# Clustered attention and two feed-forwards on one core: centroid similarities from split operands, fewer early weight conversions, and another order of feed-forward steps

## The chip, the cores and the metric

One core of a Trainium2 chip runs the whole kernel. The metric is the device time of one execution in microseconds (us); lower is better. The core has a matrix engine (TensorE, PE in the profile, with its weight loads listed apart as PEld), three engines for elementwise work (VectorE = DVE, ScalarE = ACT, GpSimd = POOL) and DMA queues that SyncE (SP) issues. TensorE accumulates into PSUM, a small memory of eight banks of 512 fp32 columns; everything else lies in SBUF.

## The reference

Shortened; all data are fp32 at the chip, except that the four weight matrices arrive as 64-bit floating-point numbers.

```
B, H, S, D = q.shape                        # 2, 8, 768, 64
q_n, k_n, c_n = (x / (norm(x) + 1e-06) for x in (q, k, centroids))   # written out in the source
q_assign = argmax(einsum('bhsd,hcd->bhsc', q_n, c_n), -1)            # 16 centroids per head
k_assign = argmax(einsum('bhsd,hcd->bhsc', k_n, c_n), -1)
scores = where(q_assign[..., :, None] == k_assign[..., None, :], q @ k.T / sqrt(D), -1e9)
attn = exp(scores - max(scores));  attn = attn / (sum(attn) + 1e-09)
x = (attn @ v) as [1536 tokens, 512]
h = x @ w_in;   x = maximum(0.01 * h, h) @ w_out                     # moe:  512 -> 2048 -> 512
h = x @ w_in2;  P = a0 + a1*h + a2*h^2 + a3*h^3;  Q = 1 + |b0|*|h| + |b1|*h^2
out = (P / (Q + 1e-06)) @ w_out2                                     # moe2: 512 -> 2048 -> 512
```

## The kernel before

**Numbers.** TensorE multiplies in a reduced form of fp32, fp32r, wherever exactness is kept another way: an operand is split into a high part (rounded to fp32r) and a low part (the rest), and a product of two fp32 matrices becomes three fp32r products: high·high, high·low and low·high. Names that end in h and l are such parts (`xh`, `xl`; `wih`, `wil`; `gh`, `gl`; `ph`, `pl`). The centroid similarities alone (`sims`, L307) are multiplied in plain fp32; each of their matmuls shows as two records in the trace.

**Attention** (`Attention.run`, about the first 281 us). Two heads make a pair, six tiles of 128 query rows a head, so a pair is 12 units and the eight pairs are 96. One iteration of the loop handles one new unit and several older ones, in fixed slots: maximum of the unit's scores on DVE (`row_max`, `nm`), normalisation of an older pair of units on POOL, two transposes into PSUM of the probabilities of the unit four iterations older (`pT` on PE), their high part on ACT (`ph`) and low part on DVE (`pl`), exponentials on ACT (`e`), scores of the next unit on PE (`s`), value products on PE (`o`, three units make a group), and at the end of a group an addition on DVE (`xf`) and, some iterations later, its split into `xh` and `xl` on POOL (`finish`).

Beside this the next pairs are prepared. Table `plan` in `prep_pieces` lists what a later pair needs, with an iteration (counted from that pair's first unit) and a slot of the iteration: loads of q and k, their transposes on PE into a PSUM tile `pa` (`trans`, L230), copies to `x` on ACT (`trans_out`, L233), splits into `hl` on POOL, similarities on PE, their copy `sv` on ACT, the maximum over the 16 centroids on DVE (`sims_max`, L335), one-hot rows, and the split of v into `vs` on POOL (`vsplit`, L394 and L395). The slots stand in the code where `go(...)` is called: "act" before the exponential, "pe" after the scores, "dve" after the low parts, "end" last. The transposes, the similarities and `pT` take turns in three PSUM tiles of one tag; two larger tiles hold scores, and one holds `o`.

**Weights.** A 64-bit weight chunk (`st`) becomes fp32 (`wf`, or `xst` in the first part of attention) by one ACT operation (`conv_a`, L767), one DVE shift (`conv_s`, L774) and two DVE combinations (`conv_c`, L780), and is then split by ACT (L787) and POOL (L790). In attention each iteration does one such small step at most, two iterations of three, for the four chunks that the first group of the first feed-forward needs (two of `wi`, two of `wo`). These chunks are saved to a DRAM scratch buffer and loaded again as plain fp32 at the end of attention.

**Feed-forwards.** 128 steps (n, j, f): a group of weights n, a block j of 384 tokens, a slice f of 128 hidden columns; steps 0 to 63 are the first (leaky), 64 to 127 the second (rational). `make_h(i)` is 12 matmuls of 384 columns into one of four `h` tiles, `back(i)` the product with `wo` into four accumulators `y0` to `y3`: 12 matmuls of 384 columns in the first feed-forward, 9 of 512 in the second. The loop body for step i does `back(i - 3)`, then `make_h(i)`, then the elementwise work of step i-1 and of i-2, then, where a block of a group ends, `collect(i - 3)`: additions on DVE that free the accumulators. In the second feed-forward the elementwise chain of a step goes ACT (`y`, `u`), POOL (`z`, twice), ACT (`ln`, `r`), DVE (`u`, `r`, `h`), ACT (`gh`), DVE (`gl`).

Engines take their instructions in the order of the program, and the order is written by hand (a manual schedule): an instruction that waits holds up what is behind it on its engine.

## Time and profile before

| | |
|---|---|
| time, three runs | 829.56, 830.09, 830.41 us (median 830.09) |
| profiled execution | 830.46 us, of which its span in the trace is 828.7 us |
| busy: PE, PEld | 797.1 us (96%), 740.7 us (89%) |
| busy: DVE, ACT, POOL | 649.1 us (78%), 533.3 us (64%), 398.8 us (48%) |
| granted TensorE clock, mean | 0.998 of full speed |
| moved by DMA | 79.80 MB, 96 GB/s over the span |

The span is cut into stretches by landmarks of the work: a pair of attention begins with the exponential of its first unit (60.67, 93.18, 124.27, ... us), the first feed-forward runs from about 281 to 545 us, the second to 825, and the last output lands at 828.7 us. Busy shares are means over stages with different limits, so the argument goes by stage. TensorE's records are pipelined: a record lasts longer than the distance to the next one, and the pace is read from the distances of starts.

### The profile page before, as it was taken

The page shows a single profiled execution, that of the slowest core. Times are in us where ns is not written, and L with a number is a line of the kernel's source. Part 1 is how long each engine was busy: PE and PEld are TensorE (multiplying, and loading weights), DVE is VectorE, ACT ScalarE, POOL GpSimd, SP SyncE. Part 2 cuts the span into 40 slices and gives each one's busy share as a digit, 9 for nine tenths or more (in the row PEclk, how much of TensorE's full clock was granted, in tenths as well). Part 3 has the DMA queues.
Part 4 walks back from the last instruction along what each step waited for, and adds up shares of the span by engine and source line. Part 5 has one row for each costly group of instructions (what it writes and reads, how often), then busy time and mean ns, then how long its engine had stood idle before and what let it go on. Part 6 is the DMA issues. An engine that isn't in the chain of part 4 may idle for free.

```text
span 828.7 us, 13356 instructions
## 1 busy us (share of the span) xinstructions
PE 797.1 (96%) x4545; PEld 740.7 (89%) x4545; DVE 649.1 (78%) x1232; ACT 533.3 (64%) x1131; POOL 398.8 (48%) x428
## 2 busy tenths in 40 slices
PE   5898999999999899999999999999999999999997
PEld 4887898898888899999999999997889888988995
DVE  6579989989999557766567556758888878888887
ACT  4588988988989544544253345447666667766664
POOL 5557877877665422331031024256555555554442
PEclk9999999999999999999999999999999999999999
DMA  3775745645410223435544454431111110100112
GB/s 102 175 207 116 169 103 117 170 97 124 106 36 26 102 85 120 131 124 169 165 147 155 141 189 130 150 89 27 35 30 28 38 39 26 26 1 1 40 39 76
DMA packets 42835, 79.80 MB, mean 96 GB/s; under 512 B 5392, under 2 KB 25360, under 8 KB 42768
## 3 DMA queue, kind: packets, MB, share of 16 engines
q1 hardware_dynamic: 42768, 78.96, 33.9%
q8 instruction: 36, 0.59, 0.3%
q14 instruction: 31, 0.25, 0.1%
HBM read 50.37 MB, written 10.49 MB: 73 GB/s over the span
## 4 chain that ended last, share of the span: by engine, by line
PE 50%; POOL 15%; DVE 14%; ACT 10%; issue 8%; DMA 2%; SPq 1%; POOLq 0%; DVEq 0%; ACTq 0%
PE y L961 18%; PE h L961 17%; POOL z L1013 6%; PE o L552 5%; PE pT L519 4%; POOL z L1010 4%; PE s L477 3%; DVE pl L538 3%; DVE nm L486 3%; ACT ln L1026 2%; PE sims L307 2%; ACT r L1027 2%; POOL wol L790 2%; POOL wil L790 2%; DMA st<-in_moe_w_in_dram 1%
## 5 line engine op out<-in xcount | busy, mean ns | idle before, releaser
L961 PE MATMUL h<-xh,wil 128*128 128x384 f32 x512 | 172.2, 336 | 0.0
L961 PE MATMUL h<-xh,wih 128*128 128x384 f32 x512 | 171.9, 336 | 0.0
L961 PE MATMUL h<-xl,wih 128*128 128x384 f32 x512 | 171.8, 336 | 0.0
L995 DVE TENSOR_TENSOR gl<-h,gh 128x384 fp32r<-128x384 f32 x128 | 70.8, 553 | 85.6 <-ACT gh L990 68.0
L511 POOL TENSOR_SCALAR e<-e,sum 128x768 f32<-128x768 f32 x96 | 88.6, 936 | 61.5 <-DVE sum L507 44.4
L790 POOL TENSOR_TENSOR wil<-wf,wih 128x512 fp32r<-128x512 f32 x32 | 41.6, 1308 | 143.8 <-ACT wih L787 143.8
L538 DVE TENSOR_TENSOR pl<-pT,ph 128x384 fp32r<-128x384 f32 x192 | 97.2, 545 | 16.6 <-ACT ph L532 15.5
L961 PEld LDWEIGHTS h<-xl,wih 128*128 128x128 f32 x512 | 96.2, 188 | 2.7
L961 PEld LDWEIGHTS h<-xh,wih 128*128 128x128 f32 x512 | 96.2, 188 | 2.5
L486 DVE TENSOR_REDUCE nm<-s 128x1 f32<-128x768 f32 x96 | 90.9, 947 | 7.3 <-PE s L477 6.8
L961 PEld LDWEIGHTS h<-xh,wil 128*128 128x128 f32 x512 | 96.2, 188 | 0.0
L999 ACT ACTIVATE h<-h 128x384 f32<-128x384 f32 x64 | 30.4, 476 | 98.6 <-PE h L961 98.6
L532 ACT CAST ph<-pT 128x384 fp32r<-128x384 f32 x192 | 82.4, 481 | 17.4 <-PE pT L519 16.2
L497 ACT ACTIVATE e<-s,nm 128x768 f32<-128x768 f32 x96 | 87.3, 909 | 9.4 <-DVE nm L486 5.8
L990 ACT CAST gh<-h 128x384 fp32r<-128x384 f32 x128 | 61.6, 482 | 40.4 <-DVE h L1034 38.3
L961 PE MATMUL y<-gh,woh 128*128 128x384 f32 x256 | 86.1, 336 | 0.1
L961 PE MATMUL y<-gl,woh 128*128 128x384 f32 x256 | 85.8, 335 | 0.2 <-DVE gl L995 0.2
L961 PE MATMUL y<-gh,wol 128*128 128x384 f32 x256 | 85.9, 336 | 0.0
L519 PE MATMUL pT<-ident,e 128*128 128x128 f32 x576 | 81.7, 278 | 2.7 <-DVE pl L538 2.7
L1010 POOL TENSOR_SCALAR z<-y,abv 128x384 f32<-128x384 f32 x64 | 43.2, 676 | 77.6 <-ACT y L1006 70.4
L961 PE MATMUL y<-woh,gh 128*128 128x512 f32 x192 | 76.6, 399 | 2.5 <-ACT gh L990 1.5
L961 PE MATMUL y<-woh,gl 128*128 128x512 f32 x192 | 76.6, 399 | 1.3 <-DVE gl L995 1.0
(104 smaller groups left out, 1855.3 us busy)
## 6 DMA issues: line engine op xcount, KB each, us to landing
st<-in_moe_w_in_dram SPq DMA_DIRECT2D x30, 512.0 KB, 4.6
st<-in_moe_w_out_dram SPq DMA_DIRECT2D x30, 512.0 KB, 4.6
a<-hl SPq DMA_DIRECT2D x56, 192.0 KB, 3.7
b<-hl SPq DMA_DIRECT2D x28, 192.0 KB, 6.0
wf<-scratch_wi SPq DMA_DIRECT2D x14, 256.0 KB, 3.1
wf<-scratch_wo SPq DMA_DIRECT2D x14, 256.0 KB, 3.1
qraw<-in_q_dram SPq DMA_DIRECT2D x16, 192.0 KB, 3.1
kraw<-in_k_dram SPq DMA_DIRECT2D x16, 192.0 KB, 3.2
```

What stands on the lines that cost most here:

```text
L486: nc.vector.reduce_max(un["nm"], un["s"][:, 0:S], axis=AX.X, negate=True)
L497: nc.scalar.activation(un["e"], un["s"][:, 0:S], AF.Exp, bias=un["nm"], accum_out=un["recip"])
L511: nc.gpsimd.tensor_scalar(un["e"], un["e"], un["recip"], 1.0, op0=ALU.mult, op1=ALU.mult)
L519: nc.tensor.transpose(pp[:, kt * P:(kt + 1) * P], un["e"][:, k0:k0 + P], ident)
L532: nc.scalar.copy(un["hi", part], un["pT", part])
L538: nc.vector.tensor_tensor(self.group[gi]["pl"][:, part * n:(part + 1) * n, i * P:(i + 1) * P], un["pT", part], f32(un["hi", part]), op=ALU ...
L790: nc.gpsimd.tensor_tensor(hold["l"][:, i:i + wr, :], hold["wf", i], f32(hold["h"][:, i:i + wr, :]), op=ALU.subtract,)
L961: nc.tensor.matmul(o, lhsT=l, rhs=r, start=(first and idx == 0), stop=(last and idx == n - 1),)
L990: nc.scalar.copy(d["gh"], d["h"])
L995: nc.vector.tensor_tensor(d["gl"], d["h"], f32(d["gh"]), op=ALU.subtract)
L1010: nc.gpsimd.tensor_scalar(d["z"], d["y"], abv[:, 1:2], abv[:, 0:1], op0=ALU.mult, op1=ALU.add)
L1013: nc.gpsimd.tensor_tensor(d["z"], d["z"], d["y"], op=ALU.mult)
```

## The change

1. **Similarities.** For the second to the eighth pair `sims` is replaced by `sims_split`: the centroids are split once into `cs` (two new POOL operations in the startup), and each of the six tiles of a head takes two fp32r matmuls: the high part of q or k against both parts of the centroids (64 columns), and its low part against the high part (32 columns, added to the first half). ACT copies 384 instead of 192 columns out of PSUM (`split_out`), and a new POOL operation adds the two halves (`add_sims`, L348). The first pair keeps plain fp32. In the second pair the maximum and the three steps behind it come one iteration later.
2. **Transposes of q and k** go to a new slot "pa", behind the value products and the low parts.
3. **Early weights.** Only the two `wi` chunks are still converted in attention and saved to scratch, one step every third iteration from the 15th on; the two `wo` chunks are loaded at the end of attention in their 64-bit form and converted there.
4. **End of attention.** The last two units have their own denominators; the last one is normalised by DVE instead of POOL, its transposes take a score tile, and the last group's `o` a tile of the tag `pT`.
5. **Feed-forward steps.** `make_h(i)` stands before `back(i - LAG)`.

```diff
--- before.py
+++ after.py
@@ -96,6 +96,7 @@
         nc.vector.tensor_tensor(abv, bv, nbv, op=ALU.max)
 
     cc = const.tile([P, H, 2, C], F32, name="cc")
+    cs = const.tile([P, H, 2, 2, C], F32R, name="cs")
 
     xh = {}
     xl = {}
@@ -189,6 +190,11 @@
+        def centroid_split(self):
+            gp = nc.gpsimd
+            gp.tensor_scalar(cs[:, :, 0], cc, 1.0, 1.0, op0=ALU.mult, op1=ALU.mult)
+            gp.tensor_tensor(cs[:, :, 1], cc, f32(cs[:, :, 0]), op=ALU.subtract)
+
         def centroid_zero(self):
             nc.gpsimd.memset(cc, 0.0)
 
@@ -312,6 +318,38 @@
                         stop=True,
                     )
 
+            def sims_split(h, tile_=self.ptile):
+                pp = tile_("sims")
+                st["pp"]["s", h] = pp
+                w = 4 * C
+                c4 = cs[:, g * HP + h].rearrange("p s u c -> p (s u c)")
+                for j in range(T):
+                    i, t = divmod(j, TH)
+                    sl = slice(t * P, (t + 1) * P)
+                    nc.tensor.matmul(
+                        pp[:, j * w:(j + 1) * w], lhsT=part(h, 0, i)[:, sl], rhs=c4,
+                        start=True, stop=False,
+                    )
+                    nc.tensor.matmul(
+                        pp[:, j * w:j * w + 2 * C], lhsT=part(h, 1, i)[:, sl], rhs=c4[:, 0:2 * C],
+                        start=False, stop=True,
+                    )
+
+            def split_out(h):
+                if h == 0:
+                    st["sv"] = tok.tile([P, HP, NS2, C], F32, tag="sv", name="sv")
+                st["s2"] = tok.tile([P, T, 2, 2 * C], F32, tag="s2", name="s2")
+                nc.scalar.copy(
+                    st["s2"],
+                    st["pp"].pop(("s", h))[:, 0:4 * C * T].rearrange("p (j s n) -> p j s n", j=T, s=2),
+                )
+
+            def add_sims(h):
+                gp.tensor_tensor(
+                    st["sv"][:, h].rearrange("p (j u) c -> p j (u c)", u=2),
+                    st["s2"][:, :, 0], st["s2"][:, :, 1], op=ALU.add,
+                )
+
             def sims_out(h):
                 if h == 0:
                     st["sv"] = tok.tile([P, HP, NS2, C], F32, tag="sv", name="sv")
@@ -398,30 +436,32 @@
             plan = [
...
-                (-23, "pe", trans, 0, 1),
+                (-23, "pa", trans, 0, 1),
...
-                (-15, "pe", sims, 1),
-                (-14, "act", sims_out, 1),
+                (-15, "pe", sims_split, 1),
+                (-14, "act", split_out, 1),
+                (-14, "end", add_sims, 1),
                 (-13, "dve", sims_max),
...
@@ -441,8 +481,9 @@
             if p == 0:
                 return []
             if p == 1:
-                late = {"sims": (-12, -10), "sims_out": (-11, -9), "sims_max": -9, "is_max": -9,
-                        "rank": -9, "first": -8, "onehot": (-7, -6)}
+                late = {"sims_split": (-12, -10), "split_out": (-11, -9),
+                        "add_sims": (-11, -9), "sims_max": -8, "is_max": -8,
+                        "rank": -8, "first": -7, "onehot": (-7, -6)}
                 done = ("load_qk", "trans", "trans_out", "split_hi", "split_lo", "place_a", "place_b")
                 moved = [
                     (-13, "end", place_b, 0),
@@ -498,21 +539,23 @@
                 un["e"], un["s"][:, 0:S], AF.Exp, bias=un["nm"], accum_out=un["recip"]
             )
 
-        def denom(self, u):
+        def denom(self, u, alone=False):
             un = self.unit[u]
-            nc.scalar.activation(un["sum"], un["sum"], AF.Identity, bias=eps)
-
-        def recip(self, u):
+            x = un["recip"] if alone else un["sum"]
+            nc.scalar.activation(x, x, AF.Identity, bias=eps)
+
+        def recip(self, u, alone=False):
             un = self.unit[u]
-            nc.vector.reciprocal(un["sum"], un["sum"])
-
-        def normalize(self, u):
+            x = un["recip"] if alone else un["sum"]
+            nc.vector.reciprocal(x, x)
+
+        def normalize(self, u, eng=nc.gpsimd):
             un = self.unit[u]
-            nc.gpsimd.tensor_scalar(un["e"], un["e"], un["recip"], 1.0, op0=ALU.mult, op1=ALU.mult)
+            eng.tensor_scalar(un["e"], un["e"], un["recip"], 1.0, op0=ALU.mult, op1=ALU.mult)
 
         def trans_p(self, u, part):
             un = self.unit[u]
-            pp = self.pq.tile([P, 512], F32, tag="pT", name="pT")
+            pp = self.ring("pT") if u == NU - 1 else self.ptile("pT")
             n = T // 2
             for kt in range(n):
                 k0 = (part * n + kt) * P
@@ -546,7 +589,10 @@
             p, h, half, _ = self.info(gi * QT)
             gr = self.group[gi]
             if a == 0:
-                gr["o"] = self.po.tile([P, BLK], F32, tag="o", name="o")
+                if (gi + 1) * QT == NU:
+                    gr["o"] = self.ptile("o")[:, 0:BLK]
+                else:
+                    gr["o"] = self.po.tile([P, BLK], F32, tag="o", name="o")
             for n in range(a, z):
                 kt, j = divmod(n, 2)
                 nc.tensor.matmul(
@@ -651,6 +697,7 @@
             assign(h0)
             for h in range(HP):
                 f0["vsplit"](h)
+            self.centroid_split()
             for h in range(HP):
                 halves(f1, h)
                 by_pool(f1, h)
@@ -681,7 +728,10 @@
                 go("dve0")
                 if 0 <= i < NU:
                     self.row_max(i)
-                if i % 2 == 0 and 0 <= i - 2 < NU:
+                if NU - 1 <= i <= NU:
+                    self.recip(i - 1, True)
+                    self.normalize(i - 1, (nc.gpsimd, nc.vector)[i - NU + 1])
+                elif i % 2 == 0 and 0 <= i - 2 < NU:
                     self.recip(i - 2)
                     self.normalize(i - 2)
                     self.normalize(i - 1)
@@ -696,7 +746,9 @@
                 go("act")
                 if 0 <= i < NU:
                     self.exp(i)
-                    if i % 2 == 1:
+                    if i >= NU - 2:
+                        self.denom(i, True)
+                    elif i % 2 == 1:
                         self.denom(i)
                 if 0 <= i + 1 < NU:
                     self.scores(i + 1)
@@ -706,6 +758,7 @@
                 if live:
                     self.lo(i - TL, 0)
                     self.lo(i - TL, 1)
+                go("pa")
                 if ok and r == QT - 1:
                     self.merge_add(gi)
                 go("dve")
@@ -713,13 +766,15 @@
                 if rd == 0 and 0 <= gd < n_groups:
                     self.finish(gd)
                 go("end")
-                if UP // 2 <= i < NU - 2 * UP and i % 3:
+                if i == UP // 2:
+                    fill[1].preload(4)
+                if UP + 3 <= i < NU - 2 * UP and i % 3 == 0:
                     fill[1].step()
                 if i == last_prep:
                     self.pc.close()
                     extra[0]()
                 elif i > last_prep:
-                    extra[1]()
+                    extra[1](i >= NU + TL)
 
     class Weights:
         def __init__(self, pools):
@@ -874,8 +929,8 @@
             else:
                 weights.add((which, n), weight_source(n, which), which, n % 2, WIDE)
 
-    def queue_scratch(n):
-        for which in ("wi", "wo"):
+    def queue_scratch(n, whiches=("wi", "wo")):
+        for which in whiches:
             src = weight_source(n, which)
             t = dram.tile([P, src.shape[1], src.shape[2] // WW], F32, name=f"scratch_{which}{n}")
             weights.add((which, n), src, which, n % 2, WIDE, store=t)
@@ -909,7 +964,7 @@
                 for j in range(NB // 2, NB):
                     slot(f"xh{j}")
                     slot(f"xl{j}")
-                queue_scratch(0)
+                queue_scratch(0, ("wi",))
 
         def open_weights(which, par, **kw):
             wpools[which, par] = wctx.enter_context(
@@ -924,8 +979,9 @@
             open_stage("wsta", side="right")
             queue_group(0)
 
-        def early_step():
-            weights.step(1)
+        def early_step(late):
+            if late or weights.waits_for(("wi", 0)):
+                weights.step(1)
 
         weights = Weights(wpools)
         with ExitStack() as actx:
@@ -1107,10 +1163,10 @@
                     if WIDE and n1 + NG - 1 > NG0 and n1 + NG - 1 < len(groups):
                         queue_scratch(n1 + NG - 1)
                     total = weights.pending()
+            if i < NS:
+                make_h(i)
             if i >= LAG:
                 back(i - LAG)
-            if i < NS:
-                make_h(i)
             if 0 <= i - 1 < NS:
                 start(i - 1)
             if 0 <= i - 2 < NS and rational(i - 2):
```

On TensorE, at the k transposes of the third pair's first head (`pa<-ident,kraw`; `s` are scores, `o` value products, `pT` probability transposes), the order before is:

```order
L477 MATMUL s<-a 128x512
L477 MATMUL s<-a 128x256
L477 MATMUL s<-b 128x512
L477 MATMUL s<-b 128x256
L230 MATMUL pa<-ident,kraw 128x128 x3
L552 MATMUL o<-ph,vs 128x384
L552 MATMUL o<-pl,vs 128x384
L552 MATMUL o<-ph,vs 128x384
L552 MATMUL o<-pl,vs 128x384
L519 MATMUL pT<-ident,e 128x128 x6
```

and of the change at the same place:

```order
L518 MATMUL s<-a 128x512
L518 MATMUL s<-a 128x256
L518 MATMUL s<-b 128x512
L518 MATMUL s<-b 128x256
L598 MATMUL o<-ph,vs 128x384
L598 MATMUL o<-pl,vs 128x384
L598 MATMUL o<-ph,vs 128x384
L598 MATMUL o<-pl,vs 128x384
L236 MATMUL pa<-ident,kraw 128x128 x3
L562 MATMUL pT<-ident,e 128x128 x6
```

The transposes now stand behind the four value products instead of ahead of them.

On POOL, in the iteration just before a pair's `sims_max` (`vs` is the split of v, `xh1` and `xl1` the split of a finished group, `e` a normalisation), the order before is:

```order
L394 TENSOR_SCALAR vs_1146<-vraw_983 128x6x64
L395 TENSOR_TENSOR vs_1146<-vraw_983,vs_1146 128x6x64
L587 TENSOR_SCALAR xh1_1178<-xf_756 128x384
L588 TENSOR_TENSOR xl1_1179<-xf_756,xh1_1178 128x384
L511 TENSOR_SCALAR e_1131<-e_1131,sum_1132 128x768
```

and of the change:

```order
L432 TENSOR_SCALAR vs_1186<-vraw_1012 128x6x64
L433 TENSOR_TENSOR vs_1186<-vraw_1012,vs_1186 128x6x64
L348 TENSOR_TENSOR sv_1035<-s2_1169 128x192
L633 TENSOR_SCALAR xh1_1218<-xf_782 128x384
L634 TENSOR_TENSOR xl1_1219<-xf_782,xh1_1218 128x384
L554 TENSOR_SCALAR e_1171<-e_1171,sum_1172 128x768
```

The new addition, whose result `sv` is what `sims_max` reads, stands behind the split of v and ahead of the split of the finished group.

On TensorE at the start of the first feed-forward, at the end of the third step's `h` (`h_3984`, in the change `h_4096`), the order before is:

```order
L961 MATMUL h_3984<-xl1_1179,wih_3492 128x384
L961 MATMUL h_3984<-xh1_1178,wil_3493 128x384
L961 MATMUL y0_4005<-gh_3977,woh_3950 128x384
L961 MATMUL y0_4005<-gl_3979,woh_3950 128x384
L961 MATMUL y0_4005<-gh_3977,wol_3951 128x384
```

and of the change:

```order
L1017 MATMUL h_4096<-xl1_1219,wih_3592 128x384
L1017 MATMUL h_4096<-xh1_1218,wil_3593 128x384
L1017 MATMUL h_4117<-xh1_1218,wih_3592 128x384
L1017 MATMUL h_4117<-xl1_1219,wih_3592 128x384
L1017 MATMUL h_4117<-xh1_1218,wil_3593 128x384
```

The fourth step's `h` now comes before the first step's `y`; the same shift by one block holds in every step that follows.

## Rows read from the trace of the kernel before

**Rows 1.** Busy time of the engines, whole span, from the page.

```profile
PE 797.1 (96%) x4545; PEld 740.7 (89%) x4545; DVE 649.1 (78%) x1232; ACT 533.3 (64%) x1131; POOL 398.8 (48%) x428
```

**Rows 2.** Windows: length; busy PE, PEld, DVE, ACT, POOL (instructions); clock, DMA, GB/s.

```profile
60.67:93.18 32.51, 30.37 (x211) 27.33 (x210) 31.13 (x57) 27.62 (x67) 24.68 (x28) 1.00 0.56 124
93.18:124.27 31.09, 30.26 (x214) 27.85 (x213) 28.22 (x52) 28.08 (x68) 23.74 (x28) 1.00 0.59 137
124.27:156.19 31.92, 30.49 (x207) 27.08 (x206) 31.15 (x58) 27.55 (x66) 23.52 (x27) 1.00 0.52 115
156.19:186.87 30.68, 29.85 (x210) 27.48 (x209) 27.84 (x52) 27.06 (x66) 24.67 (x29) 1.00 0.57 142
544.91:570.73 25.82, 24.06 (x125) 21.46 (x125) 19.23 (x30) 15.35 (x31) 17.50 (x18) 1.00 0.15 47
```

**Rows 3.** Weight loads by line: min/median/max ns, first and last start.

```profile
L307 PEld LDWEIGHTS sims<-cc,x x192: 186/192/333, 8.3 to 211.3; 128*128 128x128 f32 x192
...
L552 PEld LDWEIGHTS o<-ph,vs x192: 186/188/190, 47.5 to 280.3; 128*128 128x128 f32 x192
```

**Rows 4.** Timeline of weight loads: start us, us, then [idle before <- releaser].

```profile
85.61 1.42 PEld L307 LDWEIGHTS sims<-cc,x 128*128 128x128 f32 x12
...
89.96 0.31 PEld L477 LDWEIGHTS s<-b 80*128 80x128 f32 x2
90.31 0.19 PEld L552 LDWEIGHTS o<-ph,vs 128*128 128x128 f32 x1
90.42 0.19 PEld L552 LDWEIGHTS o<-pl,vs 128*128 128x128 f32 x1
...
94.56 0.31 PEld L477 LDWEIGHTS s<-b 80*128 80x128 f32 x2
95.36 0.31 PEld L230 LDWEIGHTS pa<-ident,kraw 128*128 128x128 f32 x3 [0.49 <-ACT x L233]
```

**Rows 5.** Waits of PE and PEld: us in total, times, longest us.

```profile
PE pa L230 <- ACT x L233: 3.5, 11, 0.5
...
PEld pa L230 <- ACT x L233: 7.0, 11, 0.8
```

**Rows 6.** Timeline of POOL, DVE and ACT around a `sims_max`.

```profile
90.29 1.02 POOL L395 TENSOR_TENSOR vs<-vraw,vs 128x384 fp32r<-128x384 f32 x1
...
91.05 0.54 DVE L335 TENSOR_REDUCE mx<-sv 128x24 f32<-128x384 f32 x1
...
91.51 0.95 DVE L486 TENSOR_REDUCE nm<-s 128x1 f32<-128x768 f32 x1
...
93.18 0.90 ACT L497 ACTIVATE e<-s,nm 128x768 f32<-128x768 f32 x1
```

**Rows 7.** Conversions during attention, grouped by line: busy us, mean ns, idle before.

```profile
L780 DVE SCALAR_TENSOR_TENSOR xst<-xst 128x512 int32<-128x512 int32 x8 | 6.4, 796 | 0.0
...
L774 DVE TENSOR_SCALAR xst<-xst 128x512 int32<-128x512 int32 x4 | 2.2, 556 | 0.0
```

**Rows 8.** Timeline of PE at the end of attention.

```profile
278.64 0.45 PE L552 MATMUL o<-ph,vs 128*128 128x384 f32 x1 [1.16 <-DVE xf L573]
```

**Rows 9.** Timeline of PE: first `y`, a block's first `y`, last step's `y`.

```profile
287.73 0.45 PE L961 MATMUL y<-gl,woh 128*128 128x384 f32 x1 [0.22 <-DVE gl L995]
...
556.28 0.47 PE L961 MATMUL y<-woh,gh 128*128 128x512 f32 x1 [0.81 <-ACT r L1027]
...
822.47 0.50 PE L961 MATMUL y<-woh,gh 128*128 128x512 f32 x1 [1.21 <-ACT gh L990]
```

**Rows 10.** Timeline of ACT, second feed-forward: the same operation two steps apart.

```profile
722.70 0.62 ACT L1026 ACTIVATE ln<-z,lnc 128x384 f32<-128x384 f32 x1
...
731.18 0.62 ACT L1026 ACTIVATE ln<-z,lnc 128x384 f32<-128x384 f32 x1
```

**Rows 11.** Chain that ended last, second feed-forward's last group: start us, us, work.

```profile
781.05 2.09 PE h L961 x12
...
789.40 2.09 PE h L961 x12
```

More of the change, by code (lines that the diff above doesn't have):

```diff
@@ L400, in prep_pieces @@
                 load_qk, load_v, trans, trans_out, x_out, direct, direct_b, split_hi, split_lo, place_a, place_b,
-                sims, sims_out, sims_max, is_max, rank, first, onehot, onehot_t, onehot_out, place_oh, vsplit,
+                sims, sims_out, sims_split, split_out, add_sims, sims_max, is_max, rank, first, onehot, onehot_t, onehot_out, place_oh, vsplit,
             )}
@@ L405, in prep_pieces @@
                 (-27, "end", load_qk),
-                (-24, "pe", trans, 0, 0),
+                (-24, "pa", trans, 0, 0),
                 (-23, "act", trans_out, 0, 0),
-                (-23, "pe", trans, 0, 1),
+                (-23, "pa", trans, 0, 1),
                 (-22, "act", trans_out, 0, 1),
                 (-22, "end", split_hi, 0),
-                (-21, "pe", trans, 1, 0),
+                (-21, "pa", trans, 1, 0),
                 (-21, "end", split_lo, 0, 0),
                 (-20, "act", trans_out, 1, 0),
-                (-20, "pe", trans, 1, 1),
+                (-20, "pa", trans, 1, 1),
                 (-20, "end", split_lo, 0, 1),
                 (-19, "act", trans_out, 1, 1),
-                (-18, "pe", sims, 0),
+                (-18, "pe", sims_split, 0),
                 (-19, "end", split_hi, 1),
-                (-17, "act", sims_out, 0),
+                (-17, "act", split_out, 0),
                 (-18, "end", split_lo, 1, 0),
                 (-18, "end", place_a, 0),
+                (-17, "end", add_sims, 0),
                 (-17, "end", split_lo, 1, 1),
-                (-15, "pe", sims, 1),
-                (-14, "act", sims_out, 1),
+                (-15, "pe", sims_split, 1),
+                (-14, "act", split_out, 1),
+                (-14, "end", add_sims, 1),
                 (-13, "dve", sims_max),
```

## The prediction

> **What bounds the kernel now.** I read the busy shares first [rows 1]: PE is busy for 96% of the span, DVE for 78%, so what shortens the time must take work or waits from PE. A share over 828.7 us mixes stages, so the windows come next [rows 2]. In each of four attention pairs PE is busy 29.85 to 30.49 us of a length of 30.68 to 32.51, at a granted clock of 1.00 (the upper level, 2.4 GHz): PE idles between 0.8 and 2.1 us a pair. The longer pairs, 32.51 and 31.92, are those in which DVE has 31 us of work and some six instructions more; the others have 28. So in attention PE leads and DVE is close behind it, above it where early weights are converted. At the start of the second feed-forward PE idles 25.82 - 24.06 = 1.76 us, the last row of that group.
>
> Then the waits [rows 5], for the idle time that the change can touch, and the timelines of single places [rows 4, 6, 8 and 9], because a sum of waits doesn't say what comes next.
>
> **Transposes moved to "pa".** Two places a pair have a `kraw` transpose that waits for ACT's copy of the tile before (of the `qraw` transposes the order moves none). The waits view gives 11 of them, 3.5 us on PE and 7.0 on PEld [rows 5]. The two differ because matmul ends are modelled, so I take the pace of the loads: after `s<-b` the next load comes 90.31 - 89.96 = 0.35 us later when nothing waits, and 95.36 - 94.56 = 0.80 at a `kraw` [rows 4]: 0.45 lost. The order has 12 such places, 12 x 0.45 = 5.4, between the two sums; I use 5.3. In the new order four value products of 384 columns stand ahead of the transpose; 12 of that size take 2.09 us [rows 11], so they cover 0.70 us against a longest wait of 0.8. The wait itself is gone. What is late next is DVE: in an undisturbed pair it works 27.84 of 30.68 us, ACT 27.06 [rows 2], and some of the regained time will be waited for at `pT` or at the scores. I take three quarters: -4.0 (0 to -5.3).
>
> **Fewer conversions in attention.** Half of the four chunks are no longer converted there: two shifts and four combinations on DVE, 2 x 0.556 + 4 x 0.796 = 4.3 us [rows 7]. The pairs with conversions last (32.51 + 31.92) / 2 = 32.2, the two without (31.09 + 30.68) / 2 = 30.9 [rows 2], so two chunks cost 1.3 us of time. One of the two such costs goes: -1.3. The other two chunks' steps are thinned to every third iteration, which could free the rest: 0 to -2.7. The `wo` chunks' 4.3 us on DVE come back at the end of attention, with their ACT parts. There PE has the `h` of four steps to do, 4 x 2.09 = 8.4 us, before it needs `wo`; without that cover they would cost up to 4.3, which I keep as an end of the next term.
>
> **Start of the feed-forward.** The first `y` waits 0.22 us for `gl` [rows 9] and stands behind `h` of a third step; now it stands behind a fourth: -0.3 (-0.6 to +4.3).
>
> **Similarities on PE.** A plain fp32 pass of 32 columns and an fp32r pass both need a weight load. The loads last 192 and 188 ns at the median [rows 3]. Twelve passes of `sims` take 1.42 us from first start to last end, so a pass comes every (1.42 - 0.19) / 11 = 0.112 us; two fp32r loads that nothing holds up come 90.42 - 90.31 = 0.11 apart [rows 4]. For 14 heads the change has 12 fp32r passes where there were 12 records: 168 at the same pace. Term 0. The bounds: no fp32r pass as short as 32 or 64 columns is in the trace. If each needed its load alone, 168 x (0.188 - 0.112) = +12.8. If only the columns counted, at 2.09 / 12 / 384 us a column [rows 11], 48 columns on average would take 0.022 and the term would be -15. I take the middle because load and pace agree in the nearest rows.
> The Trainium skill states otherwise of the loads ("TensorE: Matmul & The Clock Gate", section "Weight-path perf modes — Fast Weight Load (FWL) and DoubleRow"): a faster weight load is on when 128 weights are loaded and the type isn't FP32, with about a factor of 2 measured. By that an fp32r pass would come every 0.056 us, an estimate, and the term would be 168 x 0.056 = -9.4; the loads of 188 against 192 ns [rows 3] speak against it.
>
> **Similarities on ACT, POOL and DVE.** ACT copies 384 columns instead of 192. Another ACT operation of 384 columns lasts 0.62 us [rows 10], so each of 14 copies costs up to 0.31 more, 4.3 in all. ACT idles 3.6 us in a pair [rows 2], and the next exponential starts at 93.18, 0.72 after its `nm` (91.51 + 0.95) [rows 6]; that hides it: +0.3 (0 to +4.3).
> The new POOL addition has 192 columns; one of 384 lasts 1.02 [rows 6], so it takes 0.51, 7 us in all, where POOL works 25 of 31 us. Its place matters more. It stands behind `vs`, which ends at 90.29 + 1.02 = 91.31, so it ends at 91.82, while `sims_max`, which now reads its result, started at 91.05 [rows 6]. DVE waits 0.77. Behind it on DVE are `nm` (for which ACT's exponential has the 0.72 above as slack) and the low parts, which free the PSUM tiles of the next `pT`. Six pairs, the third to the eighth, have this: 6 x 0.8 = 4.8; the second pair's maximum was put later. Of this I take 2.0 for PE (0 to +4.8), since the slack is about as long as the wait.
>
> **End of attention.** PE waits 1.16 us for `xf` before the last group's products [rows 8], which a tile of its own removes; the normalisation that DVE takes over stands ahead of its low parts and gives back about half: -0.5 (-1.2 to +0.7, a slack like the 0.72 above used up).
>
> **Second feed-forward.** With `h` ahead of `y`, the elementwise chain may lag by one more block, 2.09 us. So the waits at the beginning of a block's products, like 0.81 at 556.28 [rows 9], go: -1.8, the window's idle time [rows 2]; bounds 0 and -1.8. Afterwards nothing changes: ACT repeats the same work after 731.18 - 722.70 = 8.48 us [rows 10], PE in its own pace after 789.40 - 781.05 = 8.35 [rows 11]. Where the chain of ACT and POOL has that period it sets the time, and an order on PE doesn't alter a period. At the end the wait of 1.21 for `gh` [rows 9] gets one more `y` block as cover, but the additions that free the accumulators come a block later as well, ahead of the last chain on DVE: 0 (-1.2 to +1.2).
>
> **Sum.** -4.0 - 1.3 - 0.3 + 0 + 0.3 + 2.0 - 0.5 - 1.8 + 0 = -5.6. Against the profiled execution's 830.46 that is 824.9; that execution lies 0.37 above the median of the runs, 830.09, so the forecast is 824.5.
>
> **The rivals.**
> - *Short passes are dear (slower).* If the pace of a 32- or 64-column fp32r pass is over 0.112 + 5.6 / 168 = 0.145 us, the kernel is slower than before; with the load alone setting it, 824.5 + 12.8 = 837.3. For it: each such pass streams less than the load lasts. Against it: that holds for the fp32 passes too, and they keep 0.112. 8%.
> - *DVE takes the wait's place.* The wait of `sims_max` passes to PE in full (+4.8 instead of +2.0), and half of the transposes' gain instead of three quarters appears (-2.7 instead of -4.0): 824.5 + 2.8 + 1.3 = 828.6. For it: DVE's 28 us in a pair of 31. Against it: the slack before the exponential. 17%.
> - *The reorder doesn't do what it says.* The waits in the second feed-forward only move by a block, and so does the one at its start: 824.5 + 1.8 + 0.3 = 826.6. For it: the chain's period of 8.48 against 8.35, by which it catches up with any lead. Against it: the idle time sits at the beginning, where the chain hasn't lagged yet. 13%.
> - *fp32r loads run faster when their products are short.* Term -9.4, of which DVE passes three quarters as above: 824.5 - 7.0 = 817.5. This is the skill's rule on the faster load, and the rows on loads speak against it. 7%.
>
> **How the numbers follow.** The forecast has 55%. Of this kernel a difference within 0.2% (1.7 us, 828.4 to 831.8) can't be told from no change. Faster by more: 52 of the forecast's 55 (three for its own spread), 13, 7, and half of the second rival's 17, since 828.6 lies at the bound: 80%. Within it: the rest of those, less a little: 10%. Slower: the first rival and 2 for the uncovered ends (+4.3 twice): 10%. The range of 8 in 10 goes from 819 to 829: it holds the forecast with its unknown sizes, the second and the third rival, and leaves out the first, the fourth and a few per cent of the forecast.
>
> **What would show it.** In the profile after: the `kraw` transposes wait under 1 us in all on PE, not 3.5; a pair without conversions takes about 30.3 us instead of 30.7 to 31.1. Twelve loads of the new similarities last about 1.4 us: at 2.2 the first rival holds, at 0.8 the fourth. DVE's `sims_max` has waits for POOL of about 0.8 us in six pairs; what PE waits at `pT` or `s` behind it tells how much passed on. The `wo` conversions end before the first `y` needs them. The window after the first feed-forward idles under 0.5 us, and the later steps of the second keep their 8.48 us. The forecast is wrong if attention doesn't end some 4 us earlier, or if the new passes don't keep 0.11.

## The result and the profile after

The changed kernel took 821.66 us, median of six runs (820.41 to 825.49), where the kernel before took 830.05: 8.4 us less by the medians, with 5.6 forecast. Taken over all runs the ratio is 0.9913, 95% interval 0.989 to 0.9936, which is 5.3 to 9.1 us less; one execution of the kernel before, of 1565.84 us, is left out of it. The next table cuts the profiled executions at landmarks (first `h` and last `y` are starts on PE).

| | before | after | |
|---|---|---|---|
| start to first `h` (attention) | 280.84 | 277.10 | -3.7 |
| first `h` to last `y` (both feed-forwards) | 543.71 | 538.41 | -5.3 |
| last `y` to the span's end | 4.15 | 4.19 | 0 |

Attention gave what the prediction's terms for it add up to (-3.5), the feed-forwards two and a half times what theirs do (-2.1). Busy shares of the profile after, answering [rows 1]:

```profile
PE 794.1 (97%) x4545; PEld 740.5 (90%) x4545; DVE 654.4 (80%) x1234; ACT 532.3 (65%) x1132; POOL 406.5 (50%) x443
```

Windows after, with the columns of [rows 2]: the five pairs from the second on, and the beginning of the second feed-forward.

```profile
59.73:90.14 30.41, 30.12 (x211) 27.59 (x210) 27.34 (x53) 28.40 (x68) 24.48 (x29) 1.00 0.57 127
90.14:121.93 31.79, 30.72 (x212) 27.73 (x211) 29.63 (x56) 27.70 (x66) 25.59 (x29) 1.00 0.53 122
121.93:153.12 31.19, 30.37 (x209) 27.30 (x207) 28.43 (x54) 27.64 (x66) 25.77 (x31) 1.00 0.49 112
153.12:183.24 30.12, 29.98 (x210) 27.57 (x209) 27.73 (x53) 27.45 (x67) 24.75 (x30) 1.00 0.61 146
183.24:213.28 30.04, 29.90 (x210) 27.58 (x209) 27.29 (x53) 27.33 (x66) 24.72 (x30) 1.00 0.56 121
...
540.70:566.50 25.80, 25.80 (x139) 24.41 (x139) 20.92 (x34) 17.08 (x35) 18.21 (x18) 1.00 0.16 54
```

The fifth pair went from 30.68 to 30.12 and PE now idles 0.14 us in it instead of 0.83. No pair has 31 us of DVE work any more. In the last row PE doesn't idle at all; it idled 1.76 us there. The first `y`, at 285.44 us, waits for nothing, so the `wo` conversions were covered.

Loads of the new similarities, answering [rows 3], and PE's timeline at one of them:

```profile
L329 PEld LDWEIGHTS sims<-cs,hl x84: 187/192/334, 26.3 to 206.7; 128*128 128x128 f32 x84
...
L333 PEld LDWEIGHTS sims<-cs,hl x84: 188/192/334, 26.5 to 206.8; 128*128 128x128 f32 x84
```

```profile
167.47 0.19 PE L329 MATMUL sims<-cs,hl 128*128 128x64 f32 x1
167.50 0.26 PE L333 MATMUL sims<-cs,hl 128*128 128x32 f32 x1
...
168.72 0.87 PE L562 MATMUL pT<-ident,e 128*128 128x128 f32 x6
```

Twelve passes take 168.72 - 167.47 = 1.25 us, 0.104 each. The loads last 192 ns at the median, as those of plain fp32 did: neither a faster load nor a dearer short pass shows. Waits of PE and of DVE after, answering [rows 5 and 6]:

```profile
PE pa L236 <- ACT x L239: 0.3, 1, 0.3
...
DVE mx L373 <- POOL sv L348: 2.5, 6, 0.9
```

The transposes' 3.5 us on PE became 0.3; the new wait of the maximum is there in all six pairs, 0.4 us on average instead of the 0.77 worked out. PE at the end of attention, answering [rows 8]:

```profile
270.32 0.55 PE L562 MATMUL pT<-ident,e 128*128 128x128 f32 x3 [1.48 <-DVE pl L581]
```

The wait of 1.16 us for `xf` is gone, and a wait of 1.48 for DVE's low parts stands a little ahead of its place. PE at the last step's `y`, answering [rows 9], and the operation of ACT two steps apart, answering [rows 10]:

```profile
813.43 0.50 PE L1017 MATMUL y<-woh,gh 128*128 128x512 f32 x1 [0.65 <-ACT gh L1046]
```

```profile
720.95 0.62 ACT L1082 ACTIVATE ln<-z,lnc 128x384 f32<-128x384 f32 x1 [1.45 <-POOL z L1069]
...
729.43 0.62 ACT L1082 ACTIVATE ln<-z,lnc 128x384 f32<-128x384 f32 x1 [1.46 <-POOL z L1069]
```

ACT's period is still 8.48 us.

### The profile page after: what moved, and what is told of

Same layout as the page of the kernel before. It is cut to its first block, busy times and chain, and to the rows that moved or that the text cites. A ratio compares the mean times of both kernels' runs of the same rounds, so it can differ in the third digit from the quotient of the medians.

```text
span 819.7 us, 13354 instructions
## 1 busy us (share of the span) xinstructions
PE 794.1 (97%) x4545; PEld 740.5 (90%) x4545; DVE 654.4 (80%) x1234; ACT 532.3 (65%) x1132; POOL 406.5 (50%) x443
## 4 chain that ended last, share of the span: by engine, by line
PE 53%; POOL 17%; DVE 12%; ACT 8%; issue 8%; DMA 1%; SPq 0%; POOLq 0%; ACTq 0%; DVEq 0%
PE h L1017 20%; PE y L1017 20%; POOL z L1069 5%; PE o L598 4%; POOL z L1066 4%; PE s L518 4%; DVE pl L581 3%; PE pT L562 3%; DVE nm L527 3%; POOL e L554 2%; POOL wol L845 2%; ACT ln L1082 2%; ACT r L1083 2%; POOL wil L845 2%; ACT y L1062 1%
## 5 line engine op out<-in xcount | busy, mean ns | idle before, releaser
L835 DVE SCALAR_TENSOR_TENSOR wf<-st,wf 128x512 int32<-128x512 int32 x124 | 83.4, 724 | 0.0
L845 POOL TENSOR_TENSOR wol<-wf,woh 128x512 fp32r<-128x512 f32 x32 | 41.9, 1323 | 71.8 <-ACT woh L842 54.7
```

What stands on the lines that cost most here:

```text
L835: nc.vector.scalar_tensor_tensor(wi, hold["st", i][:, :, :, 1 - w], sc, wi, op0=op, op1=ALU.bitwise_or)
L845: nc.gpsimd.tensor_tensor(hold["l"][:, i:i + wr, :], hold["wf", i], f32(hold["h"][:, i:i + wr, :]), op=ALU.subtract,)
```

## The experiments

Times are medians, each beside the kernel before on the same chip; its median was 829.5 to 830.4 on the three chips used. Medians of one kernel scatter by about 1 us, single runs by several (828.7 to 835.7 for the kernel before on one chip). Each kernel has one profiled execution, and in these the scatter lies in attention: from first `h` to last `y` nine kernels with the new order take 538.4 to 538.7 us. So the feed-forwards are also compared by that stretch, and a table at the end of this section gives the stretches of every kernel.

**The changed kernel again.** 

> The changed kernel once more, beside the others on one chip. Six executions of it lay between 820.4 and 825.5 us, those of the kernel before between 829.5 and 830.4. Theory A: two levels, one near 821 and one near 825, which come with nothing that the mean granted clock shows (0.995 at 825.5, 0.989 at 821.6); then this one again shows values at both. Theory B: the spread is the early stretch of lower clock, whose length differs by run; then the times go with the mean clock, and 0.01 of clock is some us.

821.73 us (821.18 to 822.61), ratio 0.9891 (0.9866 to 0.9917). No run near 825 came, and 822.61 had a mean clock of 0.987, but 821.18 had 0.990: neither theory is borne out. Theory B goes by the mean clock, and the last section shows that this misses part of the low stretch. 821.7 is the reference below.

**Feed-forward order.** The edit:

```diff
-            if i < NS:
-                make_h(i)
             if i >= LAG:
                 back(i - LAG)
+            if i < NS:
+                make_h(i)
```

> The changed kernel with one part undone: back(i - LAG) before make_h(i) again. Theory A, by the stage times of the two traces: the feed-forwards took 547.9 us before and 542.6 after, so the order alone is worth about 5 us and this takes 826 to 827. Theory B, the prediction's sizes: the order is worth 2.1 us (0.3 at the start, 1.8 at the beginning of the second feed-forward), this takes 823 to 824, and the other 3 us of the feed-forwards come from what attention leaves behind (DMA, weights done earlier).

828.99 us: 7.3 slower than 821.7. First `h` to last `y` is 544.74 us (538.67 in the changed kernel beside it). The converse, the new order alone in the kernel before:

> The kernel before with the feed-forward order alone changed. Theory A: the order is worth what undoing it cost in the changed kernel, 6 to 7.3 us, wherever attention ends: 822.5 to 824. Theory B, the prediction's size: 2.1 us, 827.7 to 828.

825.63 us, ratio 0.9934 (0.9911 to 0.9957): -4.8, and 538.40 us from first `h` to last `y` against 543.71. In both kernels the stretch moves by 5.3 to 6.1 us; theory B with 2.1 falls in both. Theory A's numbers are missed too (826 to 827, 822.5 to 824): attention ended 2.4 and 1.5 us later in these two profiled executions than in the kernels beside them. The difference of 5.3 and 6.1 is mostly one wait of the first of the two kernels:

```profile
286.81 0.44 PE L1017 MATMUL y<-gh,woh 128*128 128x384 f32 x1 [0.96 <-ACT gh L1046]
```

Its first `y` stands behind three steps of `h` again, and ACT, which now converts `wo` there, isn't ready. So in the change the fourth block of `h` covers the late `wo` too.

**Transposes.** `trans` in its old slot again, four such lines:

```diff
-                (-23, "pa", trans, 0, 1),
+                (-23, "pe", trans, 0, 1),
```

> The changed kernel with the transposes of q and k back in the slot ahead of the value products. Theory A, the prediction's term: 4.0 us slower, so 825 to 826, the kraw transposes wait some 3.5 us on PE again, and the sixth and seventh pair take 30.7 us each again instead of 30.1. Theory B: the pairs are shorter for another reason (the conversions, or similarities that no longer wait for x), then under 1.5 us slower, 821.5 to 823.

825.60 us, 3.9 slower; the first `h` starts at 280.83 instead of 276.99, and the fifth and sixth pair (the expectation counts them as sixth and seventh) take 30.9 us each instead of 30.1. The transposes wait 2.9 us on PE for `x`, nine times. Theory A.

**Similarities.** Plain fp32 for all pairs, the second pair's times as before, no `centroid_split`.

```diff
-                (-15, "pe", sims_split, 1),
-                (-14, "act", split_out, 1),
-                (-14, "end", add_sims, 1),
+                (-15, "pe", sims, 1),
+                (-14, "act", sims_out, 1),
```

> The changed kernel with plain fp32 similarities for all pairs and the second pair's maximum an iteration earlier, as before the change; the centroids aren't split. Theory A, the prediction's terms: the passes cost the same (12 in 1.3 to 1.4 us), and without the POOL addition and the larger copy this is faster by 0.3 to 2.3 us, 819.5 to 821.5. Theory B: the DVE waits of sims_max (2.5 us in the trace after, six times) have slack and cost nothing, then the same time within 1 us. Theory C: fp32r passes are really faster than the records say, then 2 us slower or more, 823.5 or above.

817.85 us, ratio 0.9841 (0.9812 to 0.9869): 3.9 faster than with split operands. PE at the same place:

```profile
165.28 1.42 PE L313 MATMUL sims<-cc,x 128*128 128x32 f32 x12
166.54 0.64 PE L559 MATMUL pT<-ident,e 128*128 128x128 f32 x4
```

1.26 us for twelve records: the passes cost the same, and what splitting costs lies elsewhere. The gain is larger than theory A's 0.3 to 2.3. This is also the fastest kernel of the study, ahead of both.

**The maximum later.**

```diff
-                (-13, "dve", sims_max),
+                (-12, "dve", sims_max),
```

> The changed kernel with sims_max one iteration later for the third to the eighth pair, so that it no longer meets an unfinished POOL addition; addition, larger copy and split products stay. Plain fp32 similarities were 3.9 us faster than the changed kernel. Theory A, the prediction's: the wait of DVE's maximum (2.3 us in five places, and what stands behind it) is that cost; then the waits are gone and the time is 818 to 819.5. Theory B: the cost is the additions on POOL and the larger copies on ACT, which delay normalisations and exponentials; then under 1 us is gained, 820.8 to 821.7.

821.44 us. DVE's wait for the POOL addition is gone from the trace (2.5 us before), and the time is the same within the scatter of about 1 us (819.08 to 824.01). Theory B: of the 2.0 us that the prediction put on this wait, less than the scatter is there.

**No addition, small copy.** `split_out` copies the first 192 columns straight into `sv`:

```diff
-                    st["s2"],
-                    ...rearrange("p (j s n) -> p j s n", j=T, s=2),
+                    st["sv"][:, h].rearrange("p (j u) c -> p j (u c)", u=2),
+                    ...rearrange("p (j s n) -> p j s n", j=T, s=2)[:, :, 0],
...
-                (-14, "end", add_sims, 1),
```

> The changed kernel with split products on TensorE, but only their first half is copied (192 columns, straight into sv) and the POOL addition is gone, so the low part of the centroids is left out of the similarities. Theory A: the 3.9 us that split similarities cost come from the addition on POOL and the larger copy on ACT, not from the passes; then 817.5 to 818.5, as with plain fp32. Theory B: they come from the passes, from their later operands (hl instead of x) or from the start of the kernel; then 820.5 to 822.

819.38 us, between the two theories: 2.35 of the 3.9 us go with the addition and the larger copy. The other 1.5, near the scatter, were not traced.

**Early weights** as before:

```diff
-                if i == UP // 2:
-                    fill[1].preload(4)
-                if UP + 3 <= i < NU - 2 * UP and i % 3 == 0:
+                if UP // 2 <= i < NU - 2 * UP and i % 3:
                     fill[1].step()
...
-                queue_scratch(0, ("wi",))
+                queue_scratch(0)
...
-            if late or weights.waits_for(("wi", 0)):
-                weights.step(1)
+            weights.step(1)
```

> The changed kernel with the early weights as before: all four chunks converted in attention, two iterations of three, the wo chunks saved and loaded again. Theory A, the prediction's term: 1.3 us slower (0 to 2.7), 823.0 with 821.7 for the changed kernel; some pair takes 1 to 2 us longer. Theory B: since the stage times leave 2.7 us of attention's 3.7 to conversions and the end of attention once transposes (-3.8) and similarities (+2.8) are taken off, the conversions are worth 2 to 2.7, 824 to 824.4.

830.59 us, 8.9 slower: outside both. The window of the fourth pair, and three rows of that kernel's DVE, ACT and PE at its end:

```profile
128.37:162.51 34.14, 31.48 (x211) 27.48 (x209) 31.94 (x58) 28.13 (x66) 25.69 (x29) 1.00 0.51 116
```

```profile
161.00 0.55 DVE L373 TENSOR_REDUCE mx<-sv 128x24 f32<-128x384 f32 x1 [1.42 <-POOL sv L348]
...
162.51 0.90 ACT L538 ACTIVATE e<-s,nm 128x768 f32<-128x768 f32 x1 [1.10 <-DVE sum L550]
...
163.09 0.92 PE L562 MATMUL pT<-ident,e 128*128 128x128 f32 x6 [1.15 <-DVE pl L581]
```

Here the wait of the maximum does reach PE: DVE has 31.94 us of work in the pair, so what it loses comes out again in the exponential and in `pT`. At the first chunk the trace shows a second cost:

```profile
51.98 0.66 ACT L820 ACTIVATE xst<-xst 128x512 f32<-128x512 f32 x1 [2.97 <-DMA xst<-in_moe_w_in_dram]
...
53.74 1.51 PE L562 MATMUL pT<-ident,e 128*128 128x128 f32 x6 [2.60 <-DVE pl L581]
```

ACT reaches the conversion before the load has landed, and PE idles behind it. Right behind that wait the granted clock is at its lower level of 1.2 GHz for 3.42 us:

```profile
53.61:57.03 3.42, 3.29 (x13) 3.22 (x14) 2.33 (x4) 2.95 (x8) 0.00 (x0) 0.50 0.64 221
```

That the wait alone brought it down is not shown: in the kernel before with split similarities PE waits 2.3 us at the same place, and no such stretch is recorded. In the changed kernel the loads start at iteration 6 and the first conversion stands at iteration 15.

**Both at once.** The last diff and that of plain similarities together.

> Two parts of the change undone together: plain fp32 similarities and the early weights as before (the transposes' slot, the end of attention and the feed-forward order stay changed). Undone alone, the early weights cost 8.9 us (830.6) and plain similarities gained 3.9 (817.9), with 821.7 for the changed kernel. Theory A: the two touch one another, since with the conversions DVE has no slack left for what split similarities add; then undoing the weights costs only the 1.3 to 2.7 us of the prediction here, 819 to 820.6. Theory B: the effects add up, 817.9 + 8.9 = 826.8.

822.00 us. With plain similarities the early weights cost 4.2 us (817.85 to 822.00), not 8.9; with the old weights splitting costs 8.6 (822.00 to 830.59), not 3.9. Neither theory's number: they touch one another by 4.7 us, but the conversions alone cost more than the pairs of before showed. ACT's wait for the first load is 1.6 us here, the second and fourth pair take 32.50 and 31.93 (30.16 and 30.51 with plain similarities and the new weights).

Where they touch is read from the two traces. Up to the second pair this kernel takes 60.6 us and the one above 65.0, so 4.4 of the 4.7 us lie there. The DMA queue with the load of the first weight chunk, in the kernel with split similarities and then here:

```profile
44.22 2.58 SPq L292 DMA_DIRECT2D a<-hl  x4
46.84 1.36 SPq L808 DMA_DIRECT2D xst<-in_moe_w_in_dram  x2
```

```profile
41.48 2.56 SPq L292 DMA_DIRECT2D a<-hl  x4
44.09 1.41 SPq L804 DMA_DIRECT2D xst<-in_moe_w_in_dram  x2
```

The load stands behind a transfer of `hl`, which POOL writes. With split similarities POOL has the additions and the second pair's later maximum ahead of that, ends this `hl` at 44.19 instead of 41.45, and the load is issued 2.75 us later. DVE's slack, theory A's reason, doesn't show there.

**Split similarities alone in the kernel before.** `centroid_split`, `sims_split`, `split_out` and `add_sims` as in the change, and in the tables:

```diff
-                (-15, "pe", sims, 1),
-                (-14, "act", sims_out, 1),
+                (-15, "pe", sims_split, 1),
+                (-14, "act", split_out, 1),
+                (-14, "end", add_sims, 1),
...
-                        "rank": -9, "first": -8, "onehot": (-7, -6)}
+                        "rank": -8, "first": -7, "onehot": (-7, -6)}
```

> The kernel before with split similarities alone (with the second pair's later maximum). Theory A: the early conversions leave DVE no slack, so this is slower by clearly more than the 3.9 us measured in the changed kernel, 837 to 841 with 829.5 before. Theory B: the cost is the same with or without conversions, 833 to 834. By the prediction's terms it would be +2.3, 832.

836.79 us, ratio 1.0071 (1.0044 to 1.0098): 6.3 slower. More than in the changed kernel, but neither theory's range; the part is a loss alone. ACT's wait for the first load is 2.7 us (1.1 in the kernel before).

**End of attention** as before:

```diff
-                if NU - 1 <= i <= NU:
-                    self.recip(i - 1, True)
-                    self.normalize(i - 1, (nc.gpsimd, nc.vector)[i - NU + 1])
-                elif i % 2 == 0 and 0 <= i - 2 < NU:
+                if i % 2 == 0 and 0 <= i - 2 < NU:
...
-            pp = self.ring("pT") if u == NU - 1 else self.ptile("pT")
+            pp = self.ptile("pT")
...
-                if (gi + 1) * QT == NU:
-                    gr["o"] = self.ptile("o")[:, 0:BLK]
-                else:
-                    gr["o"] = self.po.tile([P, BLK], F32, tag="o", name="o")
+                gr["o"] = self.po.tile([P, BLK], F32, tag="o", name="o")
```

> The changed kernel with the end of attention as before: denominators of the last two units together, the last one normalised by POOL, its transposes and the last o in their old tiles. Theory A, the prediction's term: 0.5 us slower, 821.7 + 0.5 = 822.2, bounds 821.0 to 822.9; the wait of 1.16 us for xf is back. Theory B: 1.4 us or more slower, the part of attention's gain that the conversions do not take.

822.01 us (819.32 to 822.56): no difference that can be told from 821.7. PE at the end of attention:

```profile
266.61 0.55 PE L562 MATMUL pT<-ident,e 128*128 128x128 f32 x3 [0.33 <-DVE pl L581]
...
272.44 0.44 PE L595 MATMUL o<-ph,vs 128*128 128x384 f32 x1 [1.16 <-DVE xf L616]
```

The wait for `xf` is back, and that for the low parts is 0.33 instead of 1.48 us: the change only exchanges one for the other.

**A shorter chain in the second feed-forward,** on top of plain similarities.

```diff
-            nc.gpsimd.tensor_tensor(d["z"], d["z"], d["y"], op=ALU.mult)
+            nc.vector.tensor_tensor(d["z"], d["z"], d["y"], op=ALU.mult)
```

> The kernel with plain fp32 similarities (817.9 us) in which DVE instead of POOL multiplies z by y in the second feed-forward, which takes about 0.5 us out of the chain of ACT and POOL in each of its steps. Theory A: this chain's period of 8.48 us against PE's 8.35 causes all that PE still waits from 650 to 745 us (1.2 us); then these waits go, the period falls to PE's 8.35, and the time is 816 to 817. Theory B: DVE, with 85% busy there, becomes the engine that is waited for, and the time is 818 or more.

829.23 us, 11.4 slower. The window over the same part of the feed-forward:

```profile
566.00:746.00 180.00, 174.75 (x852) 151.20 (x851) 164.31 (x315) 118.23 (x225) 53.35 (x62) 1.00 0.08 26
```

Among DVE's waits of that kernel, in us, times, longest:

```profile
DVE z L1065 <- POOL z L1062: 16.0, 20, 2.3
```

DVE is at 164 of 180 us (152.8 with the product on POOL), and the product now waits on it for POOL's half with everything else of DVE behind. PE falls from 179.77 to 174.75. Theory B, and much more than it said. Whether the chain's period alone makes PE wait is not shown by it.

**All kernels by stretch,** profiled executions, in us.

| | start to second pair | second to seventh pair | eighth pair to first `h` | first `h` to last `y` |
|---|---|---|---|---|
| before | 60.7 | 185.5 | 34.7 | 543.7 |
| feed-forward order alone in before | 61.1 | 185.9 | 35.3 | 538.4 |
| split similarities alone in before | 63.4 | 188.4 | 35.5 | 543.7 |
| changed | 59.7 | 182.2 | 35.2 | 538.4 |
| changed, again | 60.1 | 181.0 | 35.9 | 538.7 |
| old feed-forward order | 62.1 | 182.3 | 35.0 | 544.7 |
| old transposes | 60.7 | 184.8 | 35.3 | 538.4 |
| plain similarities | 59.9 | 178.5 | 35.8 | 538.5 |
| maximum later | 59.8 | 180.6 | 35.9 | 538.7 |
| no addition, small copy | 59.4 | 179.8 | 35.3 | 538.4 |
| old early weights | 65.0 | 186.0 | 35.4 | 538.7 |
| plain similarities, old weights | 60.6 | 182.4 | 34.7 | 538.4 |
| old end of attention | 57.6 | 181.6 | 35.4 | 538.7 |
| plain similarities, product on DVE | 59.6 | 178.7 | 37.1 | 548.4 |

In the second to the seventh pair the effects of weights and similarities add up. The old weights cost 3.9 us with plain similarities (182.4 - 178.5) and 3.8 to 5.0 with split ones (186.0 against 181.0 to 182.2); splitting costs 3.6 with the old weights, 2.5 to 3.7 with the new ones and 2.9 in the kernel before.

## Why the prediction was right, and where its terms were not

- **What bounds the kernel:** right. What took waits from PE gained, and the kernels with more work on DVE in a stretch (old weights, product on DVE) lost there.
- **Transposes, -4.0:** 3.9 measured, the waits of 3.5 us fell to 0.3.
- **Similarities on PE, 0:** right, 1.25 against 1.26 us for twelve passes. Both rivals on the passes' pace fall. The faster load of which the Trainium skill tells ("TensorE: Matmul & The Clock Gate", section "Weight-path perf modes — Fast Weight Load (FWL) and DoubleRow") does not show in this trace: 192 ns in either kind.
- **Similarities on ACT, POOL and DVE, +2.3:** 3.9 in this kernel, and for another reason than the one given. The wait of `sims_max` exists, but without it the time is the same within 1 us; the step that failed is "of this I take 2.0 for PE", and the rival by which this wait passes to PE in full falls with it. The addition (0.60 us) and the copy (0.50 instead of 0.33), 14 times, cost 2.35 together. Which of the two, and through what, was not separated.
- **Fewer conversions, -1.3:** between -4.2 and -8.9, the most mis-sized term by amount. The step that failed is "two chunks cost 1.3 us of time": it took the two pairs with conversions of the trace before and nothing else, and left out the first chunk, for which ACT waits (1.1 to 3.0 us in the kernels with the old weights). In the second to the seventh pair it is some 4 us with either kind of similarities; the rest of the 8.9 lies ahead of the second pair, with PE's wait of 2.6 us behind the first load and the low clock after it. Why the pairs of before showed only 1.3 each is not known.
- These two errors nearly cancel. Similarities and weights together were forecast as +2.3 - 1.3 = +1.0; undoing both gives 822.0 against 821.7, so -0.3. That attention's total came out right, -3.7 for -3.5, is luck: one part is off by 1.6 us and another by at least 2.9, in opposite directions.
- **End of attention, -0.5:** 0.3, not distinguishable from none. The step "gives back about half" is off: the wait for `xf` fell by 1.16 us and the one for DVE's low parts rose by 1.15 (0.33 to 1.48).
- **Feed-forwards, -0.3 - 1.8 + 0 = -2.1:** -5.3 by the stretch. Counted as distance of starts less PE's pace, the waits of the kernel before are 0.5 at the start, 0.3 in the first feed-forward, 2.4 in four places between 555 and 567 us, 0.9 in four between 574 and 618, and 1.8 in the tail. In the change only the tail's are left, 1.5 there, and small ones from 653 us on that both kernels have. That makes 4.4 us, and the rest lies in smaller gaps. Two steps failed.
  - "-1.8, the window's idle time". Idle is length less busy time, and a record lasts longer than the distance to the next one, so it misses a part of each wait. From 544.91 to 570.73 PE starts eleven blocks, 11 x 2.09 = 23.0 us at its own pace, so 2.8 of the 25.82 us are lost, not 1.76; "bounds 0 and -1.8" was too narrow.
  - "Afterwards nothing changes". The period is unchanged, as it said (8.48). But with `h` a block earlier the chain has 2.09 us more before its `gh` is needed, and being slower than PE by 8.48 - 8.35 = 0.13 us in two steps it would need some 30 steps to use that up, an estimate. In the changed kernel PE's first gap in the second feed-forward comes at 653 us, about 24 steps behind its first `y` at 552.7; in the kernel before there were eight by 618. The lead, from the end of a step's `gh` to the start of its `y`, shrinks meanwhile; the fifth and the 21st step:

```profile
566.38 0.48 ACT L1046 CAST gh<-h 128x384 fp32r<-128x384 f32 x1 [0.27 <-DVE h L1090]
...
569.41 0.39 PE L1017 MATMUL y<-woh,gh 128*128 128x512 f32 x1
```

```profile
634.25 0.48 ACT L1046 CAST gh<-h 128x384 fp32r<-128x384 f32 x1 [0.26 <-DVE h L1090]
636.53 0.47 PE L1017 MATMUL y<-woh,gh 128*128 128x512 f32 x1
```

  It is 2.55 and then 1.80 us, 0.09 less every two steps; in the kernel before it is 1.80 at the fifth step already. The rival by which the reorder only moves waits is wrong: the waits at the beginning are gone, and behind 653 us both kernels have the same.
- The parts as undone one by one add up to 16.5 us, not 8.4: they aren't independent (the late `wo` needs the new order, the first load waits longer with split similarities), and 1 to 2 us of each is scatter.

## What to carry to other kernels

A stage that is slower than the bounding engine by one or two per cent costs nothing until it has eaten the lead, so price a reorder by the lead that it gives and the steps that it lasts, not by the waits of one window. When two edits together don't cost the sum of both, cut the traces into stretches before blaming an engine that they share: here they added up in the pairs, and what was left over was one load, issued later behind another transfer. And when a total comes out right, undo the parts before believing them: this change contains one that is a loss of 3.9 us.

## What the runs showed that I had not expected

The granted clock in the records missed a stretch at the lower level. The windows from 25 to 30 us, of the profiled execution of the changed kernel and of the same kernel repeated beside the experiments:

```profile
25.00:30.00 5.00, 5.00 (x21) 4.66 (x20) 1.92 (x2) 1.84 (x4) 0.89 (x2) 0.50 0.14 29
```

```profile
25.00:30.00 5.00, 5.00 (x21) 4.65 (x20) 1.92 (x2) 1.83 (x4) 0.90 (x2) 1.00 0.14 29
```

The first shows 0.50, the lower level of 1.2 GHz, the second 1.00; yet instructions, busy times and the loads' 0.33 us there (0.19 later) are the same. The length of an instruction told the level, the clock column did not. How long that stretch lasts differs by execution. The next six microseconds, in the profiled execution with the old end of attention and in the repeated kernel:

```profile
30.00:36.00 6.00, 5.85 (x37) 5.26 (x36) 3.12 (x6) 4.27 (x13) 2.50 (x4) 1.00 1.02 227
```

```profile
30.00:36.00 6.00, 6.00 (x26) 5.61 (x26) 1.99 (x3) 3.02 (x8) 2.56 (x4) 1.00 1.00 226
```

Both show 1.00, but PE has 37 matmuls in the first and 26 in the second: the loads of the similarities last 0.19 us from 32.1 us on in the first, and still 0.33 up to 34.4 in the second. Up to the second pair the first takes 57.6 us and the second 60.1, and 819.32 us was the shortest time of its kernel (median 822.01). So part of the scatter in attention is this stretch.
